# Five unread products in TensorE's first pauses, and the score buffers of an attention kernel in a pool of their own

## The chip, the core and the metric

One core of a Trainium2 chip runs the whole program. Its engines are TensorE (PE in the rows; PEld is its loading of stationary operands), VectorE (DVE), ScalarE (ACT), GpSimd (POOL) and SyncE (SP), whose queue starts the transfers. The metric is the time of one execution on the device, in microseconds, as the median of several runs.

## The reference

An attention block with decay feeds two feed-forward blocks, all in fp32 (4 batches, 8 heads, 576 positions, head size 64):

```python
scores = scale * np.matmul(q, k.transpose(0, 1, 3, 2))
decay = cum[:, :, :, None] - cum[:, :, None, :]      # cum = cumsum(log(clip(f)))
scores = np.where(causal, -1000000000.0, scores + decay)
attn = softmax(scores)                               # with row maximum, + 1e-9 in the sum
x = matmul(attn, v)                                  # to 2304 tokens x 512
h = x @ w_in;  x = (h * np.cos(h)) @ w_out           # 512 -> 2048 -> 512
g = x @ w_gate; out = (silu(g) * (x @ w_val)) @ w_out2   # 512 -> 1536 -> 512
```

## The kernel before

**Attention** goes over 16 pairs of heads, with the two heads of a pair on the two halves of the partitions. The scores of a pair are made in five row tiles (`emit_s`, `S0` to `S4`, lines 311 and 314): pair 0 straight from the loaded fp32 `raw` tile, the others from a high and a low part (`xqh`, `xql`) that GpSimd splits off; a product of `sel` and `cs` adds the decay. VectorE adds the mask and takes the row maximum (`M`, line 338), ScalarE takes the exponential (`E`, line 345), TensorE transposes the result with the identity `ident` (`T`, line 382), ScalarE and VectorE copy the transposes out of PSUM (`C`, lines 390 and 392), and TensorE multiplies by `v` (`V`, line 403). VectorE scales by the reciprocal row sums into `xp` (`N`, line 414), and a transfer writes `xp` to DRAM as `x1` (line 418).

The order on every engine is a list written out by hand, `SCH`: an entry `S2@2` is step `S2` of the pair two before the one of the present round. In the first rounds most steps have no pair yet, so TensorE has nothing between the scores of pair 0 (`S0 S1 S4`, then `S2 S3`), those of pair 1 and those of pair 2. The four score tiles of PSUM are single, so `S2` waits until the maxima of `S0`, `S1` and `S4` are taken, and the next pair's `S0` until those of `S2` and `S3` are. The transposes, the product with `v`, and the two products with which the program begins (`WARM`, line 264) take their results from one pool, `ps_t`, of four PSUM buffers, in turn.

At the same time weights are loaded and turned from 64 to 32 bits and into high and low parts (`w_step`, the `stage` pool).

**The two blocks after it** work on chunks of 384 tokens. For the first, `in1` makes `h` from 12 products (`mm_in`, line 198), ScalarE rounds it to `n` (line 536), VectorE forms `a` and `r`, ScalarE takes the sine, VectorE multiplies, and `gh` and `gl` (lines 548 and 107) are its two parts; `out1` (line 563) multiplies them by the second weight, two steps behind `in1`. A chunk's input is loaded by `load_x` into `xl` and split by GpSimd into `xh` and `xl` (lines 110 and 107). The second chunk's load is held by a gate: a one-element copy from `rs` of the last pair into `xl`. The weights of this stage are still being turned while it runs.

**Memory.** Pools are stacked from the left (`wa`, then `ap1`, `ap2`, `stage` of attention) and from the right (`xpool` of the first chunk). When attention ends its pools are closed, and the next pools (`stage2`, `wb` on the left; `xpool2`, `mp2` with `n`, `mp3` with `r`, `gh`, `gl`, then `pp`, `wst` on the right) lie over the same bytes. A tile waits for the last users of the bytes under it.

Of the kernel before, what the change touches and what calls it, by code (L numbers as in the profile page):

```python
# [9 lines left out]
F32 = mybir.dt.float32  # L10
F32R = mybir.dt.float32r
# [7 lines left out]
B, H, S, D = 4, 8, 576, 64  # L19
NH = B * H  # L20
NPAIR = NH // 2
# [10 lines left out]
RWB = 3  # L32
# [3 lines left out]
WARM = 2  # L36
# [19 lines left out]
SIDE_R = "right"  # L56
# [33 lines left out]
def body(ctx: ExitStack, tc: tile.TileContext, qk, v, f, w_in, w_out, w_gate, w_val, w_out2, mask_c, ident_c, sel_c, out):  # L90
    nc = tc.nc
    PE, ACT, DVE, POOL, SP = nc.tensor, nc.scalar, nc.vector, nc.gpsimd, nc.sync
# [13 lines left out]
    def subtract(eng, o, a, b):  # L106
        eng.tensor_tensor(out=o, in0=a, in1=b.bitcast(F32), op=ALU.subtract)  # L107

    def pool_round(o, a):
        POOL.tensor_scalar(out=o, in0=a, scalar1=1.0, scalar2=0.0, op0=ALU.mult, op1=ALU.add)  # L110
# [96 lines left out]
    def load_x(pool, src, t0, n, g=False, later=False):  # L207
        xl = pool.tile([128, KD, n], F32R, tag="xl", name="xl")
        xh = pool.tile([128, KD, n], F32R, tag="xh", name="xh")
        if g:  # L210
            gate(xl[0:1, 0, 0:1])
        SP.dma_start(out=xl.bitcast(F32), in_=src[:, :, t0:t0 + n])
        for kk in range(KD):
            if later:
                xsplit.append((xh, xl, kk))
            else:
                split_x(xh, xl, kk)
        return xh, xl


    xpools = [None, None]
    xpools[0] = ctx.enter_context(tc.tile_pool(name="xpool", bufs=1, side=SIDE_R))
    actx = ExitStack()
    ap1 = actx.enter_context(tc.tile_pool(name="ap1", bufs=1))
    mask = ap1.tile([128, S], F32, name="mask")
    ident = ap1.tile([128, 128], F32, name="ident")
    ap2 = actx.enter_context(tc.tile_pool(name="ap2", bufs=2))
    stages[0] = actx.enter_context(tc.tile_pool(name="stage", bufs=2))
    pctx = ExitStack()
    ps_t = ctx.enter_context(tc.tile_pool(name="ps_t", bufs=PST, space=PSUM))  # L230
# [4 lines left out]
    raws = {}  # L235

    def load_pair(i):
        raws[i] = ap1.tile([128, 2, S], F32, tag="raw", name="raw", bufs=RWB)
        SP.dma_start(out=raws[i], in_=qk[i])

    def prep_v(i):
        vt_t[i] = ap2.tile([128, 5, 2, D], F32, tag="vt", name="vt", bufs=VTB)
        SP.dma_start(out=vt_t[i], in_=v[i])
# [4 lines left out]
    Ps = [ap1.tile([128, PW], F32, name=f"P{k}") for k in range(PB)]  # L248
    fo, lc = Ps[2:4]
    lf, ones, cum = fo[:, 0:S], fo[:, S:2 * S], lc[:, 0:S]  # L250
    cs = ap1.tile([128, S], F32R, name="cs")
    selr = ap1.tile([128, NPAIR + 1], F32, name="selr")
    sel = ap1.tile([128, NPAIR, 128], F32R, name="sel")
    SP.dma_start(out=lf, in_=f)
    load_pair(0)
    SP.dma_start(out=selr, in_=sel_c)
    SP.dma_start(out=mask, in_=mask_c)
# [1 line left out]
    SP.dma_start(out=ident, in_=ident_c)  # L259
    DVE.memset(ones, 1.0)  # L260

    for k in range(WARM):
        idle = ps_t.tile([128, 512], F32, tag="t", name="t")
        PE.matmul(idle, lhsT=ones[:, 0:128], rhs=ones[:, 0:512], start=True, stop=True)
    DVE.memset(hpi, float(np.pi / 2))
    ACT.activation(out=hpi[:, 0:1], in_=ones[:, 0:1], func=AF.Ln)
    ACT.activation(out=hpi[:, 0:1], in_=ones[:, 0:1], func=AF.Identity, scale=float(np.pi / 2))
# [20 lines left out]
    xq = {}  # L288

    def emit_q(i, k):  # L290

        if k == 0:
            xq[i] = [ap2.tile([128, 2, S], F32R, tag=a, name=a) for a in ("xqh", "xql")]
        (h, l), x = xq[i], raws[i]
        if k % 2 == 0:
            pool_round(h[:, k // 2], x[:, k // 2])
        else:
            subtract(POOL, l[:, k // 2], x[:, k // 2], h[:, k // 2])

    def s_mm(i, t, at, lo, n):  # L300

        q0, rows, _, _ = QT[t]
        if i:
            xh, xl = xq[i]
            parts = (xh, xh), (xl, xh), (xh, xl)
        else:
            parts = (raws[i], raws[i]),
        for m, (x, y) in enumerate(parts):
            for e in range(2):
                b = slice(64 * e, 64 * e + 64)  # L310
                PE.matmul(ss[e][:rows, at[0], at[1]], lhsT=x[b, 0, q0:q0 + rows], rhs=y[b, 1, lo:lo + n], start=(m == 0), stop=False)  # L311
        for e in range(2):
            b = slice(64 * e, 64 * e + 64)
            PE.matmul(ss[e][:rows, at[0], at[1]], lhsT=sel[b, i, :rows], rhs=cs[b, lo:lo + n], start=False, stop=True)  # L314

    def emit_s(i, t):
        if t == 4:
            for h in range(2):
                s_mm(i, 4, (h, slice(0, 288)), 288 * h, 288)
        else:  # L320
            s_mm(i, t, SAT[t], 0, QT[t][2])
# [11 lines left out]
    def emit_m(p, t):  # L333
        if p not in P:
            P[p] = Ps[p % PB]
        q0, rows, ext, c0 = QT[t]
        m1 = S if t else S - 64
        DVE.tensor_tensor_reduce(  # L338
            out=view(P[p][:rows, c0:c0 + ext], t), in0=ss[p % 2][:rows, SAT[t][0], SAT[t][1]], in1=view(mask[:rows, m1 - ext:m1], t),
            scale=-0.125, scalar=3e38, op0=ALU.add, op1=ALU.min, accum_out=mxt[p % 8][:rows, t:t + 1])  # L340

    def emit_e(p, t):
        q0, rows, ext, c0 = QT[t]
        o = P[p][:rows, c0:c0 + ext]
        ACT.activation(out=o, in_=o, func=AF.Exp, scale=-1.0, bias=mxt[p % 8][:rows, t:t + 1],  # L345
                       accum_out=smt[p // 2 % 3][:rows, p % 2, t:t + 1])
# [30 lines left out]
    def emit_t(p, b):  # L377
        ps = tps[p, b] = ps_t.tile([128, 512], F32, tag="t", name="t")
        for col, t, j in TB[b]:
            q0, rows, ext, c0 = QT[t]  # L380
            k0 = c0 + k_lo(j)
            PE.transpose(ps[:, col:col + 128], in_=P[p][:, k0:k0 + 128], identity=ident)  # L382

    def emit_c(p, b):
        if p not in PT:
            PT[p] = ap2.tile([128, PTW], F32, tag="pt", name="pt", bufs=PTB)
        ps = tps.pop((p, b))
        o = PT[p][:, TB_OFF[b]:TB_OFF[b] + TB_W[b]]
        if PTE[p % 2][b]:
            DVE.tensor_copy(o, ps[:, :TB_W[b]])  # L390
        else:
            ACT.copy(out=o, in_=ps[:, :TB_W[b]])  # L392
# [4 lines left out]
    def emit_pv(i, half):  # L397

        q0, w, blocks = PVH[half]
        ps = pvs[i, half] = ps_t.tile([128, 512], F32, tag="t", name="t")  # L400
        for j, c, o in blocks:
            for e in range(2):
                PE.matmul(ps[64 * e:64 * e + 64, o:w], lhsT=vt_t[i][:, j, e], rhs=PT[2 * i + e][:, c:c + w - o],  # L403
                          start=(j == 0), stop=(j == blocks[-1][0]))
# [11 lines left out]
    def emit_o(i):  # L416
        b, hp = divmod(i, H // 2)
        SP.dma_start(out=x1[128 * hp:128 * hp + 128, S * b:S * b + S], in_=xp.pop(i))
# [6 lines left out]
    def load_chunk(k, later=False):  # L425
        if k < len(chunks):
            s, c = chunks[k]
            xs[s, c] = load_x(xpools[k % 2], x1v if s == 1 else x2v, c * CH, CH, GX and k == 1, later)

    def op(o, i):  # L430

        if not 0 <= i < NPAIR:
            return
        k, e = o[0], int(o[-1]) if o[-1] in "01" else 0
        p = 2 * i + e
        if o[:2] == "ld":
            i > 1 and load_pair(i)
        elif o == "lv":
            prep_v(i)
        elif k == "S":  # L440
            emit_s(i, int(o[1]))
        elif k == "M":
            emit_m(p, int(o[1]))
        elif k == "E":
            emit_e(p, int(o[1]))
        elif k == "T":
            emit_t(p, int(o[1]))
        elif k == "C":
            emit_c(p, int(o[1]))
        elif k == "r":  # L450
            emit_recip(i, o[1])
        elif k == "V":
            emit_pv(i, e)
        elif k == "N":
            emit_n(i, e)
        elif o == "xo":
            emit_o(i)
        elif o == "xk":
            if i == XL:
                load_chunk(0, True)  # L460
            elif i >= XP:
                for _ in range(min(XN, len(xsplit))):
                    split_x(*xsplit.pop(0))
        elif o == "wd":
            i < SA and w_load(i)
        elif k == "w":
            i < SA and w_step(i, int(o[1]))
        elif k == "q":
            i and emit_q(i, int(o[1]))
        else:  # L470
            raise ValueError(o)
# [29 lines left out]


    rctx = ExitStack()
    xpools[1] = rctx.enter_context(tc.tile_pool(name="xpool2", bufs=1, side=SIDE_R))
    mp2 = rctx.enter_context(tc.tile_pool(name="mp2", bufs=2, side=SIDE_R))
    mp3 = rctx.enter_context(tc.tile_pool(name="mp3", bufs=3, side=SIDE_R))
    pctx2 = ExitStack()
    pp = pctx2.enter_context(tc.tile_pool(name="pp", bufs=1, side=SIDE_R))
    wst = pctx2.enter_context(tc.tile_pool(name="wst", bufs=2, side=SIDE_R))
# [121 lines left out]
    for i in range(len(steps) + LAG):  # L631
        if i < len(steps):
# [7 lines left out]
            k = chunks.index((s, c)) + 1  # L640
# [103 lines left out]
```

## Time and profile before

| | us |
|---|---|
| median of 3 runs | 1048.92 (1047.85 to 1051.23) |
| the profiled execution | 1050.59 |
| its span, first to last instruction | 1048.8 |
| TensorE busy in it | 1030.2 (98%) |

Attention takes about the first 192 us, the first block runs to about 595 us, the second to the end. The rows quoted below are of one profiled execution; times in them start at the first instruction.

### The profile page before, as it was taken

To read this page: it belongs to the slowest core of one execution; us is meant where nothing else is said; L and a number is where in the kernel's file an instruction comes from. 1 tells how busy PE (TensorE), PEld (TensorE's weight loads), DVE (VectorE), ACT (ScalarE), POOL (GpSimd) and SP (SyncE) were. 2 spreads that over 40 slices of the span, in tenths; PEclk is the share of its full clock that TensorE was granted. 3 is DMA by queue.
4 is the path that set the end of the run, shared out by engine and by line. 5 is a ranking of instruction groups with operands and counts; after the bars stand their busy time and mean duration, and the time that the engine had idled before them with its cause. 6 is when DMAs were issued, how large, how long until landed. Compare 5 with 4: busy or idle time off the path is not lost.

```text
span 1048.8 us, 16876 instructions
## 1 busy us (share of the span) xinstructions
PE 1030.2 (98%) x6448; PEld 964.9 (92%) x6448; DVE 548.6 (52%) x1261; ACT 436.2 (42%) x1019; POOL 314.1 (30%) x332
## 2 busy tenths in 40 slices
PE   6999999899999999999999999999999999999998
PEld 4787877799999999999999999999999999999997
DVE  4788887698898788888855411211111211111111
ACT  5888888355655555555543311111111211211211
POOL 3565655242242141321402211311311311311111
PEclk8999999999999999999999999999999999999999
DMA  4566664533465545555368630100100100000000
GB/s 156 188 187 210 189 196 144 169 107 105 161 212 204 187 154 189 191 188 172 143 231 290 235 128 1 61 1 1 61 1 1 61 1 28 34 1 1 31 1 31
DMA packets 44817, 121.91 MB, mean 116 GB/s; under 512 B 4512, under 2 KB 16064, under 8 KB 44736
## 3 DMA queue, kind: packets, MB, share of 16 engines
q1 hardware_dynamic: 44736, 120.83, 34.2%
q8 instruction: 51, 0.84, 0.3%
q14 instruction: 30, 0.25, 0.1%
HBM read 86.12 MB, written 34.68 MB: 115 GB/s over the span
## 4 chain that ended last, share of the span: by engine, by line
PE 94%; DVE 2%; ACT 2%; DMA 1%; POOL 1%; issue 0%; SPq 0%; ACTq 0%
PE h L198 46%; PE t L563 16%; PE t L597 14%; PE t L382 5%; PE s L311 4%; PE t L403 4%; PE t L566 2%; PE s L314 1%; DMA vt<-in_v_dram 1%; ACT P L345 1%; DVE P L338 0%; DMA selr<-in_sel_dram 0%; DMA x<-xp 0%; DVE r L542 0%; ACT pt L392 0%
## 5 line engine op out<-in xcount | busy, mean ns | idle before, releaser
L198 PE MATMUL h<-xh,w 128*128 128x384 f32 x1920 | 374.4, 336 | 0.5 <-POOL xh L110 0.5
L198 PEld LDWEIGHTS h<-xh,w 128*128 128x128 f32 x1920 | 338.9, 188 | 7.4 <-POOL xh L110 0.8
L198 PE MATMUL h<-xl,w 128*128 128x384 f32 x960 | 205.1, 334 | 0.0
L585 DVE TENSOR_TENSOR r<-h,r 128x384 f32<-128x384 f32 x72 | 40.1, 557 | 289.8 <-ACT r L584 289.8
L107 POOL TENSOR_TENSOR gl<-r,gh 128x384 fp32r<-128x384 f32 x72 | 72.7, 1010 | 333.5 <-ACT gh L520 333.5
L198 PEld LDWEIGHTS h<-xl,w 128*128 128x128 f32 x960 | 169.8, 188 | 0.0
L563 PE MATMUL t<-gh,w 128*128 128x384 f32 x704 | 136.5, 334 | 1.6 <-ACT gh L548 1.6
L597 PE MATMUL t<-w,gh 128*128 128x512 f32 x432 | 134.1, 392 | 0.0
L563 PEld LDWEIGHTS t<-gh,w 128*128 128x128 f32 x704 | 123.3, 188 | 2.0 <-ACT gh L548 2.0
L584 ACT ACTIVATE r<-h 128x384 f32<-128x384 f32 x72 | 35.4, 492 | 213.0 <-PE h L198 203.6
L544 ACT ACTIVATE r<-r,hpi 128x384 f32<-128x384 f32 x96 | 59.3, 618 | 125.1 <-DVE r L542 123.9
L520 ACT CAST gh<-r 128x384 fp32r<-128x384 f32 x72 | 36.9, 513 | 150.5 <-DVE r L586 150.5
L107 POOL TENSOR_TENSOR wst<-ta,wst 128x512 fp32r<-128x512 f32 x36 | 46.5, 1292 | 154.0 <-ACT wst L173 97.9
L597 PEld LDWEIGHTS t<-w,gh 128*128 128x128 f32 x432 | 80.1, 188 | 13.3
L345 ACT ACTIVATE P<-P,mx 128x576 f32<-128x576 f32 (+4 forms) x160 | 87.5, 547 | 5.7 <-DVE mx L338 5.7
L597 PE MATMUL t<-w,gl 128*128 128x512 f32 x216 | 85.2, 396 | 0.0
L540 DVE SCALAR_TENSOR_TENSOR a<-n,h 128x384 f32<-128x384 int32 x96 | 53.9, 562 | 57.9 <-ACT n L536 56.9
L338 DVE CUSTOM_DVE_ANT_0 P<-s,mask 128x576 f32<-128x576 f32 (+4 forms) x160 | 68.2, 483 | 17.0 <-PE s L314 17.0
L536 ACT ACTIVATE n<-h 128x384 int32<-128x384 f32 x96 | 47.1, 490 | 68.4 <-PE h L198 56.7
L586 DVE TENSOR_TENSOR r<-h,r 128x384 f32<-128x384 f32 x72 | 40.2, 558 | 67.4 <-PE h L198 67.4
L563 PE MATMUL t<-gl,w 128*128 128x384 f32 x352 | 75.2, 334 | 0.0
L563 PEld LDWEIGHTS t<-gl,w 128*128 128x128 f32 x352 | 62.3, 188 | 0.0
(80 smaller groups left out, 1320.3 us busy)
## 6 DMA issues: line engine op xcount, KB each, us to landing
w_d<-wst SPq DMA_DIRECT2D x36, 512.0 KB
w<-w_d SPq DMA_DIRECT2D x36, 512.0 KB
wraw<-in_w_out_dram SPq DMA_DIRECT2D x28, 512.0 KB
raw<-in_qk_dram SPq DMA_DIRECT2D x16, 576.0 KB
xl<-x SPq DMA_DIRECT2D x12, 768.0 KB
wraw<-in_w_in_dram SPq DMA_DIRECT2D x16, 512.0 KB
x<-part SPq DMA_DIRECT2D x8, 768.0 KB
wraw<-in_w_gate_dram SPq DMA_DIRECT2D x12, 512.0 KB
```

What stands on the lines that cost most here:

```text
L107: eng.tensor_tensor(out=o, in0=a, in1=b.bitcast(F32), op=ALU.subtract)
L198: PE.matmul(ps, lhsT=w[:, a, 128 * kk:128 * kk + 128], rhs=b[:, kk], start=(n == 0), stop=(n == 3 * KD - 1))
L311: PE.matmul(ss[e][:rows, at[0], at[1]], lhsT=x[b, 0, q0:q0 + rows], rhs=y[b, 1, lo:lo + n], start=(m == 0), stop=False)
L338: DVE.tensor_tensor_reduce(out=view(P[p][:rows, c0:c0 + ext], t), in0=ss[p % 2][:rows, SAT[t][0], SAT[t][1]], in1=view(mask[:rows, m1 - ex ...
L345: ACT.activation(out=o, in_=o, func=AF.Exp, scale=-1.0, bias=mxt[p % 8][:rows, t:t + 1], accum_out=smt[p // 2 % 3][:rows, p % 2, t:t + 1])
L382: PE.transpose(ps[:, col:col + 128], in_=P[p][:, k0:k0 + 128], identity=ident)
L403: PE.matmul(ps[64 * e:64 * e + 64, o:w], lhsT=vt_t[i][:, j, e], rhs=PT[2 * i + e][:, c:c + w - o], start=(j == 0), stop=(j == blocks[-1][0]))
L536: ACT.activation(out=n, in_=h, func=AF.Copy, scale=INV2PI, bias=0.25)
L540: DVE.scalar_tensor_tensor(out=a, in0=n, scalar=-PI2_HI, in1=h, op0=ALU.mult, op1=ALU.add)
L544: ACT.activation(out=r, in_=r, func=AF.Sin, bias=hpi, scale=1.0)
L563: PE.matmul(acc[m][:, :CH], lhsT=wo[:, q, 128 * m:128 * m + 128], rhs=x, start=(j == a and n == 0), stop=False)
L597: PE.matmul(acc[m], lhsT=a[:, s], rhs=w[:, b], start=(j == 0 and n == 0), stop=(j == J2 - 1 and n == 2))
```

## The change

The helper `warm` makes products whose results nobody reads. It replaces the loop of the two first products, and is called in addition after three steps of the scores: one product after `S4` of pair 0, two after `S3` of pair 0, two after `S3` of pair 1. The new products have the identity as stationary operand and 448 columns of the mask as moving one, and are fp32. `mask`, `raw`, `cs`, `selr`, `sel`, `xqh` and `xql` move from `ap1` and `ap2` into a new pool `aps`, stacked behind `ap2`; their sizes and numbers stay. On the right `mp2` and `mp3` are taken before `xpool2` and no longer after it.

```diff
     ap1 = actx.enter_context(tc.tile_pool(name="ap1", bufs=1))
-    mask = ap1.tile([128, S], F32, name="mask")
     ident = ap1.tile([128, 128], F32, name="ident")
     ap2 = actx.enter_context(tc.tile_pool(name="ap2", bufs=2))
+
+    aps = actx.enter_context(tc.tile_pool(name="aps", bufs=1))
+    mask = aps.tile([128, S], F32, name="mask")
     stages[0] = actx.enter_context(tc.tile_pool(name="stage", bufs=2))
...
-        raws[i] = ap1.tile([128, 2, S], F32, tag="raw", name="raw", bufs=RWB)
+        raws[i] = aps.tile([128, 2, S], F32, tag="raw", name="raw", bufs=RWB)
...
-    cs = ap1.tile([128, S], F32R, name="cs")
-    selr = ap1.tile([128, NPAIR + 1], F32, name="selr")
-    sel = ap1.tile([128, NPAIR, 128], F32R, name="sel")
+    cs = aps.tile([128, S], F32R, name="cs")
+    selr = aps.tile([128, NPAIR + 1], F32, name="selr")
+    sel = aps.tile([128, NPAIR, 128], F32R, name="sel")
...
-    for k in range(WARM):
-        idle = ps_t.tile([128, 512], F32, tag="t", name="t")
-        PE.matmul(idle, lhsT=ones[:, 0:128], rhs=ones[:, 0:512], start=True, stop=True)
+    def warm(n, a, b):
+        for k in range(n):
+            idle = ps_t.tile([128, 512], F32, tag="t", name="t")[:, :b.shape[-1]]
+            PE.matmul(idle, lhsT=a, rhs=b, start=True, stop=True)
+
+    warm(WARM, ones[:, 0:128], ones[:, 0:512])
...
-            xq[i] = [ap2.tile([128, 2, S], F32R, tag=a, name=a) for a in ("xqh", "xql")]
+            xq[i] = [aps.tile([128, 2, S], F32R, tag=a, name=a, bufs=2) for a in ("xqh", "xql")]
...
+    WAIT = {("S4", 0): 1, ("S3", 0): 2, ("S3", 1): 2}
+
     def op(o, i):
...
             emit_s(i, int(o[1]))
+            warm(WAIT.get((o, i), 0), ident, mask[:, 0:448])
...
     rctx = ExitStack()
-    xpools[1] = rctx.enter_context(tc.tile_pool(name="xpool2", bufs=1, side=SIDE_R))
     mp2 = rctx.enter_context(tc.tile_pool(name="mp2", bufs=2, side=SIDE_R))
     mp3 = rctx.enter_context(tc.tile_pool(name="mp3", bufs=3, side=SIDE_R))
+    xpools[1] = rctx.enter_context(tc.tile_pool(name="xpool2", bufs=1, side=SIDE_R))
```

## Rows read from the trace of the kernel before

**Rows 1.** The page: span, and the granted clock in 40 slices

```profile
span 1048.8 us, 16876 instructions
...
PEclk8999999999999999999999999999999999999999
```

**Rows 2.** What TensorE waited for: us in total, times, longest us

```profile
PE s L311 <- DVE mx L338: 4.5, 2, 2.4
PE s L311 <- POOL xql L107: 2.2, 1, 2.2
...
PE t L563 <- ACT gh L548: 1.6, 1, 1.6
...
PE h L198 <- POOL xh L110: 0.5, 1, 0.5
```

**Rows 3.** Windows of 1 us: engines' busy time, granted clock, DMA share, GB/s

```profile
14.00:15.00 1.00, 1.00 (x8) 0.64 (x6) 0.00 (x0) 0.85 (x4) 0.92 (x2) 0.60 0.52 97
...
24.00:25.00 1.00, 1.00 (x9) 0.96 (x8) 0.48 (x4) 0.81 (x2) 0.00 (x0) 0.78 0.09 16
...
31.00:32.00 1.00, 1.00 (x15) 1.00 (x15) 0.62 (x2) 1.00 (x4) 0.00 (x0) 0.63 0.07 10
...
34.00:35.00 1.00, 1.00 (x8) 1.00 (x7) 1.00 (x7) 0.45 (x1) 1.00 (x2) 0.66 0.03 12
```

**Rows 4.** TensorE's timeline: start, us, instruction, count [idle before it, releaser]

```profile
1.50 3.78 PE L264 MATMUL t<-P 128*128 128x512 f32 x4 [1.50 <-DVE hpi L265]
...
13.51 0.81 PE L311 MATMUL s<-raw 64*128 64x320 f32 x4 [2.36 <-DVE mx L338]
...
18.62 0.32 PE L311 MATMUL s<-xqh 64*64 64x64 f32 x2 [2.17 <-DVE mx L338]
...
30.63 0.24 PE L311 MATMUL s<-xqh 64*64 64x64 f32 x2 [2.18 <-POOL xql L107]
```

**Rows 5.** The chain that ended last, 0 to 45 us: start, us, what

```profile
9.93 0.24 PE s L314 x2
...
14.59 1.49 PE s L311 x4
...
20.99 0.24 PE s L314 x2
...
22.19 2.46 PE t L382 x11
...
24.76 2.10 PE t L382 x19
...
44.47 0.13 PE s L314 x2
```

**Rows 6.** VectorE's timeline, 29 to 33 us

```profile
30.40 0.08 DVE L338 DVE_READ_ACCUMULATOR2_ANT mx<- 128x1 f32 x1
...
31.00 0.62 DVE L390 COPY pt<-t 128x448 f32<-128x448 f32 x1
```

**Rows 7.** ScalarE's timeline, 23 to 33 us, first copy and last exponential

```profile
23.06 0.48 ACT L392 COPY pt<-t 128x384 f32<-128x384 f32 x1 [2.78 <-PE t L382]
...
32.60 0.18 ACT L345 ACTIVATION_READ_ACCUMULATOR P<-P,mx 128x1 f32 x1
```

**Rows 8.** ScalarE's timeline and the chain, 190 to 200 us

```profile
195.73 0.49 ACT L536 ACTIVATE n<-h 128x384 int32<-128x384 f32 x1 [11.75 <-DMA x<-xp]
...
192.44 3.19 DMA x<-xp
...
198.69 0.49 ACT gh L548
```

**Rows 9.** TensorE's timeline, 193 to 200 us

```profile
193.25 1.55 PE L198 MATMUL h<-xh,w 128*128 128x384 f32 x8
...
199.22 1.68 PE L563 MATMUL t<-gh,w 128*128 128x384 f32 x8 [1.65 <-ACT gh L548]
```

**Rows 10.** GpSimd's timeline, its last weight work of attention

```profile
188.02 1.27 POOL L107 TENSOR_TENSOR w<-ta,w 128x512 fp32r<-128x512 f32 x1
```

## The prediction

> **What bounds the kernel now.** The page first: the span is 1048.8 us and the row of TensorE's granted clock is at its top in every slice but the first [rows 1]. The profiled execution took 1050.59 us, 1.8 us more than its span; the three timed runs have a median of 1048.92 us, 1.67 us under it, and lie 3.4 us apart. The list of what TensorE waited for shows how little idle time is left: two pauses of together 4.5 us after VectorE's row maxima, one of 2.2 us put down to GpSimd, 1.6 us after ScalarE's `gh`, 0.5 us after GpSimd's `xh` [rows 2]. The first three lie in the first 31 us (2.36 us before 13.51, 2.17 us before 18.62, 2.18 us before 30.63) [rows 4]. They are the pauses that the change fills; the last two lie where attention ends.
>
> [...] The first 10 us print 1.00, but the durations say otherwise: a 288-column step of `cs` takes 0.24 us at 9.93, as it does at 20.99 under 0.50, and 0.13 at 44.47 under 1.00 [rows 5]. So the program starts at the lower level, and the record begins later.
>
> The third pause is put down to GpSimd's `xql`, but VectorE's last maximum of the second pair ends at 30.48, 0.15 us before TensorE starts at 30.63 [rows 4, 6], as in the two pauses that are put down to VectorE. All three pauses are VectorE's work on scores; its length doesn't depend on TensorE's clock, so a pause stays as long when TensorE is faster.
>
> **The change: what the products cost.** Each is an fp32 product of 448 columns; there is one after the large scores of pair 0, two after the last scores of pair 0, two after those of pair 1. [...] The products write buffers of the transposes' pool of four. In the third pause the two oldest are those of the third- and fourth-last transposed blocks; the copy that is late, on VectorE at 31.0 [rows 6], belongs to the last block and isn't theirs. [...]
>
> **What the clock gives back.** If a pause is mostly work, the fall after it should not come. From 14.2 to 16.45 the rest of pair 0's scores ran at half speed (the 448-column step alone 1.49 us, [rows 5]): 2.25 us, of which half, 1.1, comes back. From 18.62 to 24.4 TensorE worked 5.8 us at half speed, pair 1's scores and the first transposes (11 of them took 2.46 us, the 19 across and after the rise 2.10, [rows 5]): 2.9 back. From 31.3 to 34.7 3.4 us: 1.7 back. Sum 5.7 us.
>
> What is late next: ScalarE. Its copies of pair 0's transposes and then its exponentials of pair 1 run nearly unbroken from 23.06 to 32.78 [rows 7], 9.7 us. Its first copy would start at about 19.8 (1.1 us earlier by pair 0's scores, 1.75 by pair 1's, 0.45 by a block transposed at full speed) and the last exponential end at 29.5 at the latest. TensorE, which got to pair 2's scores at 30.63, gets there at 26.6, and with 1.9 to 2.0 us for them at full speed to the transposes that need that exponential at 28.6. So between 0 and 0.9 us is given back there; since part of ScalarE's 9.7 us is waiting for transposes at half speed, I take 0.4: 5.7 - 0.4 = 5.3 us. After that the chain of waits is TensorE's alone to the end of attention, so what is won early is kept. Bounds: 5.7 if ScalarE gives nothing back, 0 if the clock takes no notice.
>
> **What the new order of the buffers gives.** This is no cost of an instruction but of who lies where. Attention's pools are closed and the next stage's tiles are put over them. Adding up the sizes, the first `n` tile of the first product stage lies over the end of the last `xp` buffer, by some 480 bytes. The trace agrees: ScalarE stands still for 11.75 us until `x<-xp` has landed and starts `n` at 195.73, with the transfer from 192.44 on [rows 8], though the 12 products that make its input ended at about 193.3, where the next group starts [rows 9]. From `n` to `gh` (198.69 to 199.17) it is 3.4 us, and TensorE stands 1.65 us until 199.22 [rows 8, 9]. With `mp2` and `mp3` taken first from the right, `n`, `r`, `gh` and `gl` come over the weight staging and the end of the score pool: the last user of the first is GpSimd's `w` at 188.02 to 189.29 [rows 10], of the second the last pair's scores, made before all of that pair's transposes. Then `n` starts at about 193.35, `gh` is there at 196.8, before TensorE has run out of products at 197.57, and the 1.65 us are gone. The 0.5 us behind `xh` [rows 2] is a piece of the second chunk that GpSimd splits behind weight work which VectorE and ScalarE hand it; with these 2.4 us earlier and TensorE only 1.65 earlier, it goes too. The second chunk's tile moves over the score buffers, free far earlier, but its load is still held by the gate copy from `rs`, so it can't run into the last transfers of attention. The queue of SP keeps its order. Sum 2.1 us; bounds 0 (another late tile under `n` or `r`) and 2.1. I take 2.1, since every wait that I can name under the new places ends 4 us before `n`.
>
> Sum: 1050.59 - 5.3 - 2.1 = 1043.2 us, 0.55% under the median of the three runs. A measurement of this kernel can tell about 0.3%, 3.1 us; faster begins at 1045.8.
>
> [...]
>
> **The rivals.**
> A, the forecast: the clock is up from the first pause on, and `n` no longer waits: 1043.2 us.
> [...]
> C: the buffers give nothing, because a tile that I count as free is not: 1050.59 - 5.3 = 1045.3 us. Against: the releases listed above.
> [...]
>
> **How the numbers follow.** A 0.52, B 0.18, C 0.13, D 0.10, and 0.07 for what I haven't thought of. The predicted time is A's, 1043.2; its own range is 1041.0 to 1045.0. Lowest: all terms at their upper bounds, 5.7 + 2.1, give 1042.8, and if the timed runs lie 1.7 under the profiled one as they do now, 1041.1; so 1041.0. Highest: B with its whole overrun and C's zero, 1050.59 - 3.1 = 1047.5. That holds A, B and C, over 8 in 10, and leaves D out. Faster by over 0.3%: nearly all of A, most of B and C, 0.70. Slower by over 0.3% would need D and a bad term besides, 0.03. Within 0.3%: 0.27.
>
> **What would show it.** Right: granted clock 1.00 in every step from 11 to 45 us; three groups of 2, 4 and 4 records of the mask product, each ending before VectorE's last maximum; the unbroken stretch of TensorE starting near 17.4 and 26.6 instead of 18.62 and 30.63; `n` starting where the first product group ends, no wait of `out1` for `gh`. [...] A wait of the transposes for ScalarE of more than 0.4 us near 28 would lower the first term.

## The result, and the profile after

| | before | changed |
|---|---|---|
| median, us | 1049.97 (4 runs, 1047.85 to 1051.23) | 1041.23 (4 runs, 1040.24 to 1042.31) |
| ratio, 95% interval | | 0.9917 (0.9901 to 0.9932) |
| the profiled execution, us | 1050.59 | 1040.93 |
| its span, us | 1048.8 | 1039.1 |

The kernel became 8.7 us faster by the medians, 9.7 us by the spans of the two profiles. The forecast was 1043.2 us; the time lies at the lower end of the range, which begins at 1041.0. Over all the runs that were made beside the experiments below, the kernel before has 64 more times, with medians of 1048.6 to 1049.8 us.

What TensorE waited for, of the lines of [rows 2]: the three pauses are down from 6.7 to 1.5 us, and the lines for `gh` and `xh` are gone.

```profile
PE s L316 <- DVE mx L343: 1.0, 2, 0.5
...
PE s L316 <- POOL xql L107: 0.5, 1, 0.5
```

TensorE's timeline of the changed kernel (start, us, instruction, count, in brackets the idle time before it), beside [rows 4]:

```profile
7.53 0.24 PE L319 MATMUL s<-cs,sel 64*64 64x64 f32 x2 [1.96 <-ACT sel L284]
...
10.09 1.86 PE L267 MATMUL t<-mask,ident 128*128 128x448 f32 x2
12.47 0.81 PE L316 MATMUL s<-raw 64*128 64x320 f32 x4 [0.52 <-DVE mx L343]
...
14.31 1.77 PE L267 MATMUL t<-mask,ident 128*128 128x448 f32 x4
16.56 0.24 PE L316 MATMUL s<-xqh 64*64 64x64 f32 x2 [0.48 <-DVE mx L343]
...
23.70 1.77 PE L267 MATMUL t<-mask,ident 128*128 128x448 f32 x4
25.95 0.24 PE L316 MATMUL s<-xqh 64*64 64x64 f32 x2 [0.48 <-POOL xql L107]
...
33.08 3.35 PE L408 MATMUL t<-pt,vt 128*64 128x256 f32 x32
```

One product took 1.86 us at the lower level, two took 1.77 us at the upper one, and each group ends about 0.5 us before the work that the pause waits for. So in this profile the products lie wholly under VectorE's maxima.

The granted clock of the changed kernel in windows of 1 us (engines' busy time, clock, DMA share, GB/s), beside [rows 3]: it is at half only from 8.7 to 12.1 us, and in every later step up to 45 us it is 1.00, where the kernel before has 0.50 for 10 and for 3.4 us. The fall at 8.7 stands behind one more pause, the 1.96 us of waiting for `sel` early in the first scores (before 7.53), which the change leaves as it is. So the clock was already at half when the product of the first pause began, and it came up just behind that product.

```profile
8.00:9.00 1.00, 1.00 (x13) 0.95 (x12) 0.34 (x1) 0.72 (x1) 0.01 (x1) 0.87 0.99 401
...
12.00:13.00 1.00, 0.53 (x6) 0.46 (x6) 0.41 (x4) 0.83 (x3) 1.00 (x1) 0.93 0.00 0
...
14.00:15.00 1.00, 1.00 (x6) 0.49 (x3) 0.58 (x3) 0.05 (x1) 1.00 (x1) 1.00 0.65 166
...
24.00:25.00 1.00, 1.00 (x4) 0.38 (x2) 1.00 (x5) 1.00 (x5) 0.92 (x2) 1.00 1.05 354
...
31.00:32.00 1.00, 1.00 (x12) 0.83 (x11) 0.96 (x3) 1.00 (x4) 0.12 (x1) 1.00 0.48 90
```

The end of attention, in ScalarE's timeline, beside [rows 8]: `n` now waits for TensorE's products, not for a transfer.

```profile
186.36 0.49 ACT L545 ACTIVATE n<-h 128x384 int32<-128x384 f32 x1 [8.45 <-PE h L198]
...
189.31 0.48 ACT L557 CAST gh<-h 128x384 fp32r<-128x384 f32 x1 [0.25 <-DVE h L555]
```

And in TensorE's, beside [rows 9]: the first product of `out1` follows the last `h` without an idle bracket.

```profile
189.49 0.85 PE L198 MATMUL h<-xl,w 128*128 128x384 f32 x4
190.19 1.55 PE L572 MATMUL t<-gh,w 128*128 128x384 f32 x8
```

### The profile page after: what moved, and what is told of

Read it like the earlier page. It is cut to its first block, busy times and chain, and to the rows that moved or that the text cites. A ratio compares the mean times of both kernels' runs of the same rounds, so it can differ in the third digit from the quotient of the medians.

```text
span 1039.1 us, 16892 instructions
## 1 busy us (share of the span) xinstructions
PE 1028.8 (99%) x6458; PEld 960.9 (92%) x6458; DVE 547.0 (53%) x1261; ACT 435.9 (42%) x1019; POOL 314.4 (30%) x332
## 3 DMA queue, kind: packets, MB, share of 16 engines
q1 hardware_dynamic: 44736, 120.83, 34.7%
## 4 chain that ended last, share of the span: by engine, by line
PE 97%; ACT 1%; DVE 0%; DMA 0%; POOL 0%; issue 0%; SPq 0%; ACTq 0%
PE h L198 48%; PE t L572 18%; PE t L606 14%; PE t L387 5%; PE t L408 5%; PE s L316 4%; PE t L575 2%; PE s L319 1%; ACT P L350 1%; DVE P L343 0%; DMA selr<-in_sel_dram 0%; ACT pt L397 0%; ACT sel L284 0%; PE t L366 0%; POOL xql L107 0%
```

## The experiments

Each was timed in alternation with the kernel before; kernels of one group ran on the same chip. Ratios are to the kernel before. Eleven runs were made in three groups, one of them of the changed kernel again.

**First group: the two parts apart, and the two halves of the second part.** Median of the kernel before: 1049.84 us over 33 runs.

The products alone, every buffer where it was:

```diff
+    WAIT = {("S4", 0): 1, ("S3", 0): 2, ("S3", 1): 2}
...
             emit_s(i, int(o[1]))
+            warm(WAIT.get((o, i), 0), ident, mask[:, 0:448])
```

> The five products alone, all buffers where they were before. My theory: the products keep TensorE's clock up and are worth 5 to 6 us, so about 1044.5 us against a median of about 1050 before; granted clock 1.00 from the first pause to 45 us; ScalarE's first n still starts only when the last x<-xp has landed, and TensorE still stands about 1.6 us for gh. Rival (the start's chance and the buffers make the difference, the products little): within 2 us of the kernel before.

Measured: 1045.07 us over 10 runs, ratio 0.9966 (0.9954 to 0.9977), so 3.6 us by the ratio and 4.8 by the medians, a little less than the 5 to 6 us expected. The clock is up from 11.9 us, in the first pause, to 45 us, as expected. Its end of attention is worse than that of the kernel before: ScalarE's timeline has `n` behind the transfer still,

```profile
189.20 0.49 ACT L543 ACTIVATE n<-h 128x384 int32<-128x384 f32 x1 [11.21 <-DMA x<-xp]
```

TensorE's timeline has a longer wait than [rows 9], 2.24 us against 1.65, and a slow group behind it, 2.87 us for eight products that take 1.55 us in the changed kernel:

```profile
192.69 2.87 PE L570 MATMUL t<-gh,w 128*128 128x384 f32 x8 [2.24 <-ACT gh L555]
195.35 1.26 PE L570 MATMUL t<-gl,w 128*128 128x384 f32 x4
```

The windows show why: in this execution the longer wait is one more pause behind which the clock fell, from 192.8 to 196.2 us.

```profile
191.00:192.00 1.00, 0.00 (x0) 0.00 (x0) 0.44 (x1) 0.90 (x2) 0.00 (x0) 1.00 0.00 0
192.00:193.00 1.00, 0.31 (x1) 0.31 (x2) 0.92 (x3) 0.48 (x1) 0.00 (x0) 0.90 0.66 123
193.00:194.00 1.00, 1.00 (x4) 1.00 (x4) 0.69 (x2) 0.28 (x1) 0.00 (x0) 0.50 1.03 381
...
196.00:197.00 1.00, 1.00 (x7) 1.00 (x7) 1.00 (x3) 0.00 (x0) 0.92 (x2) 0.90 0.00 0
```

The new places of the buffers alone:

```diff
-    WAIT = {("S4", 0): 1, ("S3", 0): 2, ("S3", 1): 2}
+    WAIT = {}
```

> The new places of the buffers alone, no new product. My theory: 2.1 us for n and xh, and up to 1.1 us more if the wait of the last product with v for vt is gone because of the places: 1047 to 1048 us; the three pauses and the half-speed stretches behind them as before. Rival (the wait for vt went by chance of the queue): 2 us and a wait for vt of about 1 us still there.

Measured: 1047.75 us over 11 runs, ratio 0.9977 (0.9966 to 0.9987): 2.1 us by the medians, 2.4 by the ratio, as expected. TensorE's timeline has the three pauses of before, and a wait for `vt`:

```profile
13.32 0.90 PE L316 MATMUL s<-raw 64*128 64x320 f32 x4 [2.35 <-DVE mx L343]
...
18.52 0.32 PE L316 MATMUL s<-xqh 64*64 64x64 f32 x2 [2.17 <-DVE mx L343]
...
30.45 0.24 PE L316 MATMUL s<-xqh 64*64 64x64 f32 x2 [2.18 <-POOL xql L107]
...
188.22 3.35 PE L408 MATMUL t<-pt,vt 128*64 128x256 f32 x32 [0.90 <-DMA vt<-in_v_dram]
```

Only the order on the right, with the score buffers back in `ap1` and `ap2`, no product:

```diff
-    xpools[1] = rctx.enter_context(tc.tile_pool(name="xpool2", bufs=1, side=SIDE_R))
     mp2 = rctx.enter_context(tc.tile_pool(name="mp2", bufs=2, side=SIDE_R))
     mp3 = rctx.enter_context(tc.tile_pool(name="mp3", bufs=3, side=SIDE_R))
+    xpools[1] = rctx.enter_context(tc.tile_pool(name="xpool2", bufs=1, side=SIDE_R))
```

> Only the order of the pools on the right is changed; score buffers stay in ap1 and ap2, no product. By the bytes, n now lies over the weight staging and starts as soon as its products end, but the first r lies over the last xp buffer: VectorE's r then waits for x<-xp, and TensorE's wait for gh shrinks from 1.65 to about 0.4 us: 1.2 us won. Rival (the order of the pools is what counts, whatever lies under them): the whole 2 us.

Measured: 1048.98 us over 11 runs, ratio 0.9994 (0.9983 to 1.0004): 0.9 us by the medians where 1.2 were expected, and not clear of nothing by the ratio. Where the wait went is read from the trace. VectorE's timeline, which had no such wait in the kernel before, has `r` behind the transfer:

```profile
192.59 0.56 DVE L547 SCALAR_TENSOR_TENSOR a<-n,h 128x384 f32<-128x384 int32 x1 [1.71 <-ACT n L543]
193.92 0.56 DVE L549 SCALAR_TENSOR_TENSOR r<-n,a 128x384 f32<-128x384 int32 x1 [0.76 <-DMA x<-xp]
```

and TensorE's wait before `out1` is 0.33 us (about 0.4 expected):

```profile
196.39 1.62 PE L570 MATMUL t<-gh,w 128*128 128x384 f32 x8 [0.33 <-issue]
```

By the addresses, the wait went from the tile that lay on the end of `xp` to the next tile that lies there, `r`, 0.76 us: here the bytes counted, not the order of the pools.

Only the score buffers' own pool, the order on the right as before, no product:

```diff
     rctx = ExitStack()
+    xpools[1] = rctx.enter_context(tc.tile_pool(name="xpool2", bufs=1, side=SIDE_R))
     mp2 = rctx.enter_context(tc.tile_pool(name="mp2", bufs=2, side=SIDE_R))
     mp3 = rctx.enter_context(tc.tile_pool(name="mp3", bufs=3, side=SIDE_R))
-    xpools[1] = rctx.enter_context(tc.tile_pool(name="xpool2", bufs=1, side=SIDE_R))
...
+    WAIT = {}
```

(a diff to the changed kernel).

> Only the score buffers' own pool, the order on the right as before, no product. By the bytes, n, r, gh and gl now lie over score buffers and weight staging, nothing late: the whole 2.1 us, no wait of n for a transfer. Rival (the order of the pools is what counts): n waits for x<-xp as before, nothing won.

Measured: 1047.63 us over 11 runs, ratio 0.9982 (0.9971 to 0.9994): 2.2 us by the medians, the same as both halves together. ScalarE's timeline:

```profile
193.59 0.49 ACT L545 ACTIVATE n<-h 128x384 int32<-128x384 f32 x1 [9.59 <-PE h L198]
```

So the pool alone takes the wait away; the new order on the right adds nothing measurable to it.

**Second group: what the products have to be.** Median of the kernel before: 1048.64 us over 17 runs. Diffs are to the changed kernel.

Products of 8 columns:

```diff
-            warm(WAIT.get((o, i), 0), ident, mask[:, 0:448])
+            warm(WAIT.get((o, i), 0), ident, mask[:, 0:8])
```

> The changed kernel with the five products 8 columns wide instead of 448: as many instructions, hardly any work in the pauses. My theory (work in the pauses holds the clock): the clock falls behind the first and third pause as in the kernel before, three pauses of 2.2 to 2.4 us, 1046 to 1048 us. Rival (it is enough that TensorE issues something in the pause): clock at 1.00 and 1042 to 1043 us. Beside it, for the 1 us wait of the last product with v for vt: if it hangs on where TensorE's instructions lie in the program, it is gone here; if it hangs on how early attention ends, it is there as in the kernel before.

Measured: 1046.42 us over 12 runs, ratio 0.9977 (0.9967 to 0.9987), the ratio of the new buffers without any product. In its profile the clock fell at 8.4 us, as it did at 8.7 and 8.3 in the two profiles of the changed kernel, but it came up again at 22.0 instead of 12.1 and 11.7. The windows behind the first pause and at the rise:

```profile
13.00:14.00 1.00, 1.00 (x6) 0.70 (x6) 0.00 (x0) 1.00 (x5) 0.92 (x3) 0.50 0.00 0
...
21.00:22.00 1.00, 1.00 (x10) 0.83 (x8) 0.00 (x0) 0.00 (x0) 0.92 (x2) 0.50 0.00 0
22.00:23.00 1.00, 1.00 (x10) 0.91 (x9) 0.82 (x3) 0.32 (x1) 0.84 (x1) 0.99 0.06 16
```

The expected fall behind the third pause did not come in this profile. With as many instructions in the pauses as the changed kernel, but less work in them (0.59 us instead of 1.86 in the first), this kernel took about 5 us longer, and its clock was at half for 10 us more. The wait for `vt` was there, 1.5 us, with as many instructions as in the changed kernel, so the place of instructions in the program isn't what removes it.

No product in the first pause:

```diff
-    WAIT = {("S4", 0): 1, ("S3", 0): 2, ("S3", 1): 2}
+    WAIT = {("S3", 0): 2, ("S3", 1): 2}
```

> The changed kernel without the product in the first pause; two in the second and two in the third stay. My theory: the first pause is idle for 2.36 us and the clock falls or stays low behind it in most runs; pair 0's last scores run at half speed, the two products in the second pause start at half speed and overrun it by up to 1.1 us; the clock is up from about 17 to 20 us on: 1043 to 1044 us. Rival (one product of 0.8 to 1.7 us in the first pause does nothing): 1041.2 us like the changed kernel.

Measured: 1043.17 us over 6 runs, ratio 0.9951 (0.9937 to 0.9965). TensorE's timeline: the pause, and the two products behind it that start at half speed, 2.52 us instead of 1.77:

```profile
11.84 0.81 PE L316 MATMUL s<-raw 64*128 64x320 f32 x4 [2.34 <-DVE mx L343]
...
14.57 2.52 PE L267 MATMUL t<-mask,ident 128*128 128x448 f32 x4
```

The clock fell at 12.7 and was up at 16.1, a little earlier than I had put it; 1.7 to 1.9 us slower than the changed kernel by the medians, within the 1043 to 1044 us expected.

Twice as many products:

```diff
+    WAIT = {("S4", 0): 2, ("S3", 0): 4, ("S3", 1): 4}
```

> Twice as many products, 2, 4 and 4. At full speed a pair took 1.77 us in the changed kernel and left 0.48 us of the pause; four take 3.5 us and overrun by 1.3 us in the second and third pause each, two in the first take 1.8 to 3.7 us against 2.4 us: 0 to 1.3. My theory (the pauses are the cover of the products): 2.6 to 3.9 us slower than the changed kernel, 1044 to 1045 us, the clock as in it. Rival (VectorE or ScalarE hide the overrun, since they set the pace early on): within 1 us of the changed kernel.

Measured: 1043.41 us over 6 runs, ratio 0.995 (0.9936 to 0.9963), 1.9 to 2.2 us slower than the changed kernel. TensorE's timeline has the next scores directly behind the products, 3.21 us after the products' start where it was 2.25, so 0.96 us of overrun in the second pause and as much in the third:

```profile
13.81 3.27 PE L267 MATMUL t<-mask,ident 128*128 128x448 f32 x8
17.02 0.24 PE L316 MATMUL s<-xqh 64*64 64x64 f32 x2
```

The overrun goes into the time about one for one: in the profiles 1.9 us of it, less the 0.5 by which the second scores of pair 0 begin earlier here (11.97 against 12.47), stand against spans 1.3 us apart. It is smaller than expected because four products in a row took 3.27 us here, not twice 1.77.

Three products at the very start and two in the first pause:

```diff
-WARM = 2
+WARM = 3
...
-    WAIT = {("S4", 0): 1, ("S3", 0): 2, ("S3", 1): 2}
+    WAIT = {("S4", 0): 2, ("S3", 0): 2, ("S3", 1): 2}
```

> The changed kernel with three products at the very start instead of two, and two in the first pause instead of one. The third takes 1.7 us at half speed and ends at about 7.0 us, before the first scores' operand is there at 7.5 us, so it costs nothing. My theory: the clock is up before pair 0's scores, which then take 1.8 instead of 2.5 to 3.5 us: 0.5 to 1.5 us faster than the changed kernel, about 1040 us, with less spread. Rival (the scores wait for VectorE and ScalarE at the start, or the clock comes up no earlier): within 0.5 us of the changed kernel.

Measured: 1040.27 us over 6 runs, ratio 0.9921 (0.9908 to 0.9935), and all six within 0.28 us, 1040.11 to 1040.39. TensorE's timeline: the third product ends before the scores' operand is there, and the scores that took until 10.09 in the changed kernel's first profile end at 9.4. The wait for `sel` before 7.53, behind which the clock fell there, is filled.

```profile
1.50 5.49 PE L267 MATMUL t<-P 128*128 128x512 f32 x6 [1.50 <-DVE hpi L270]
...
9.40 1.77 PE L267 MATMUL t<-mask,ident 128*128 128x448 f32 x4
```

It is the fastest kernel here, 1.0 to 1.2 us under the medians of the changed one. The intervals of the ratios overlap, since those carry the spread of the kernel before; its own six times lie under all five of the changed kernel's in the third group, and under three of its first four (the fourth, 1040.24, lies among them).

**Third group: the changed kernel again, and two parts left out.** Median of the kernel before: 1048.78 us over 14 runs.

> The changed kernel once more, beside the two below on one chip: 1041 to 1042 us, ratio 0.991 to 0.993; in its profile the clock stays up from the first pause on, and TensorE has no wait for gh. Open beforehand: whether the last product with v waits for vt (it did in six of the ten profiles so far, 0.8 to 1.5 us, the changed kernel's not among them). If the missing wait belongs to the change, it is missing again; if it is chance, it may be there.

Measured: 1041.5 us over 5 runs (1041.17 to 1042.05), ratio 0.9929 (0.9914 to 0.9944). The clock is up from 11.7 us on; no wait for `gh`, none for `vt`.

No products in the third pause:

```diff
+    WAIT = {("S4", 0): 1, ("S3", 0): 2}
```

> The changed kernel without the two products in the third pause. My theory: TensorE idles 2.2 us there, the clock falls behind it in most runs, and pair 2's scores and the transposes behind them run 3.4 us at half speed: 0 to 1.7 us slower than the changed kernel, 1042.5 us in the middle, with more spread. Rival (after ten us of unbroken work the clock no longer falls): the same as the changed kernel.

Measured: 1044.18 us over 6 runs (1042.9 to 1044.71), ratio 0.9951 (0.9936 to 0.9966), 2.7 us slower than the changed kernel, more than expected. Its profile doesn't show what I meant to see: the third pause is there in TensorE's timeline,

```profile
13.56 1.44 PE L316 MATMUL s<-raw 64*128 64x320 f32 x4 [0.55 <-DVE mx L343]
...
17.05 1.77 PE L267 MATMUL t<-mask,ident 128*128 128x448 f32 x4
...
28.68 0.24 PE L316 MATMUL s<-xqh 64*64 64x64 f32 x2 [2.18 <-POOL xql L107]
...
30.62 1.42 PE L387 MATMUL t<-ident,P 128*128 128x128 f32 x11
```

but the 11 transposes behind it take 1.42 us, as at full speed in the changed kernel. In this execution (1044.71 us) the loss lies elsewhere, and three pieces make up the 3.8 us between the spans. The first scores ran at half speed, so that the second ones begin at 13.56 instead of 12.47: 1.1 us. Pair 0's last scores ran at half speed too, to 17.05, 3.49 us instead of 1.84: 1.65 us. And the last product with `v` waited 1.0 us for `vt`. The record of the granted clock prints 1.00 all the while; the durations show the half speed (0.81 us for the four 320-column products at 12.47 in the changed kernel, 1.44 here). Up to the third pause this kernel is the changed one, so the product in the first pause doesn't bring the clock up early in every execution. Whether the other five executions fell to half speed behind the third pause isn't known, so this run doesn't settle what that pause is worth.

Three products at the start, none in the pauses:

```diff
-WARM = 2
+WARM = 3
...
+    WAIT = {}
```

> The new buffers, three products at the very start, none in the pauses. My theory: pair 0's first scores run at full speed (1 to 1.5 us won), but the first pause is idle for 2.4 us, the clock falls behind it, and the half-speed stretches come as before: 1046 to 1047 us, 5 to 6 us behind the kernel with products at the start and in the pauses. Rival (once up, the clock stays up): 1041 us.

Measured: 1045.26 us over 8 runs (1042.73 to 1046.93), ratio 0.9964 (0.9951 to 0.9977), 5.0 us behind the kernel with products at the start and in the pauses, and a little under the 1046 to 1047 us expected. The windows show a fall at 17.3, behind the second pause, and one at 27.5, behind the third:

```profile
17.00:18.00 1.00, 1.00 (x14) 1.00 (x14) 0.00 (x0) 0.73 (x3) 0.19 (x1) 0.64 0.33 131
...
27.00:28.00 1.00, 1.00 (x18) 1.00 (x20) 0.96 (x2) 1.00 (x5) 0.00 (x0) 0.76 0.08 15
28.00:29.00 1.00, 1.00 (x12) 1.00 (x12) 0.00 (x0) 1.00 (x4) 0.00 (x0) 0.50 0.47 70
```

The first pause, 2.34 us idle, let it pass this time. So the clock, up in the first scores (192 columns of `cs` in 0.38 us at 7.96, where the kernel before took 0.64 at 8.27), didn't stay up without the products; it fell behind the second and the third pause, where the profile before has its falls behind the first and the third, at 14.2 and 31.3.

## Why the prediction was right, step by step

Case A came, with the sign, the mechanisms and the range right and the size 2 us short. The two profiles are compared stretch by stretch: 1.0 us at the start, 5.2 from there to the first product with `v`, 1.0 from there to the last one, where the wait for `vt` is gone, and 2.4 at the end of attention, together the 9.7 us of the spans. One sign was missed: the clock was to be at 1.00 from 11 us on and is so from 12.1.

**The products cost nothing: right.** By the two 512-column products at half speed, 3.78 us in [rows 4], my estimate was 1.89 x 448 / 512 = 1.65 us for one at half speed and as much for two at full speed; they took 1.86 and 1.77, 13% and 7% more, and still ended inside the pauses. Where the doubled products overran two pauses by 0.96 us each, the kernel was 1.9 to 2.2 us slower. The 1.1 us of overrun in the sum for the upper end of the range (two at half speed, 3.3 us by the same estimate, in 2.17) no run shows: the two that began at half speed, in the run without the first product, took 2.52 us, and the next scores began 2.45 us after their start, where it was 2.25 in the changed kernel.

**The clock gives back 5.3 us: right, 5.2 measured.** In the profile before it fell at 14.2 and 31.3, 0.7 us after the pauses that end at 13.51 and 30.63, and was at half to 24.4 and 34.7. From the second scores of pair 0 to the first product with `v` it was 25.8 us (13.51 to 39.31) and is 20.6 (12.47 to 33.08). Its end before, in TensorE's timeline:

```profile
39.31 3.35 PE L403 MATMUL t<-pt,vt 128*64 128x256 f32 x32
```

By pieces: pair 0's last scores 2.94 to 1.84 us, 1.1 as forecast; pair 1's scores and transposes 9.83 to 7.14, 2.7 instead of 2.9; pair 2's stretch 8.68 to 7.13, 1.55 instead of 1.7; each of the last two pauses 0.07 longer. The 0.4 us that ScalarE should have kept back weren't: its copies start at 19.07 and its exponentials end at 28.07, 9.0 us against 9.7 in [rows 7], while TensorE starts the transposes at 27.87 without a wait of its own. The two misses cancel. For the third pause the evidence is a count: none of the six profiles with full products there has a fall behind it, and five of the seven without have one (the other two are those of 8 columns and of no products in the third pause).

The second of those rises, at 34.7, came 3.4 us after the fall, but TensorE had worked without a pause for 4.1 us by then, from 30.63 on; the first, at 24.4, came after 5.8 us, from 18.62 on. In case B, with the clock at half behind the first pause, the rise would by these two come between 17.6 and 19.3 us, 4.1 to 5.8 after 13.51 (an estimate).

**The buffers give 2.1 us: right.** 2.1 us alone by the medians; in the profiles the stretch from the end of the last product with `v` to the products that finish the first partial sum (lines 566 and 575) is 37.5 us before and 35.1 after, 2.4. The pair of half changes agrees with the reason: in each of these kernels the tile that waits for the transfer is the one that by the addresses lies over `xp`, and with the score buffers in a pool of their own neither `n` nor `r` waits for it. The 0.5 us for `xh` are less sure: the wait is gone in both profiles of the changed kernel and with the buffers alone, but stands with 0.3 us in the run with products at the start only, which has the same buffers.

**What the sum left out.** Two things that the two profiles differ in besides. First, 1.0 us at the very start: the second scores of pair 0 begin at 12.47 instead of 13.51, because the first scores, which lie before any new product, ran partly at full speed in this execution. That looks like chance and not the change: in the second profile of the changed kernel they begin at 12.96, without products in the third pause at 13.56, and in that of `right_order_only`, which has no product, at 11.68. Second, 1.1 us: the last product with `v` no longer waits for `vt`. In TensorE's timelines, before and changed:

```profile
188.47 3.35 PE L403 MATMUL t<-pt,vt 128*64 128x256 f32 x32 [1.08 <-DMA vt<-in_v_dram]
...
181.23 3.35 PE L408 MATMUL t<-pt,vt 128*64 128x256 f32 x32
```

I had this line before me in the list of waits and left it out of the sum as untouched. It is absent from both profiles of the changed kernel and of the three others that have full products in all three pauses, and present (0.7 to 1.5 us) in the eight others. It doesn't hang on the buffers and not on the count of instructions; what brings the transfer in time isn't settled. It is issued no earlier: in both kernels 1.15 us before the last but one group of products with `v` begins (182.51 before 183.66, 176.42 before 177.57). It is the transfer itself that takes less, 4.8 us at most instead of 5.8.

That the time still fell inside the range, 0.2 us above its lower end, is in part luck. That end allowed for timed runs 1.7 us under the profiled one; after the change the median is 0.3 us above it, and these two unforecast gains took the place of the allowance.

**The two parts together.** Apart they give 0.9966 and 0.9977, together 0.9917 and 0.9929, some 1.5 to 2.7 us more than the product of the two, 0.9943. By the intervals only the larger of the two is clear of the noise, and barely, so that the parts help each other is likely and not shown by the times. One profile shows a way in which they could. The products alone bring attention's end forward, but `n` keeps waiting for `x<-xp`, TensorE's wait grows to 2.24 us, and in that profile the clock fell behind it. I had added the terms as independent.

**The rivals.** B has the clock fall behind the first pause in spite of its product, which by the estimate above fills 0.83 us of 2.36 at full speed. That shows in neither profile of the changed kernel. But B isn't refuted. In both profiles the clock was at half already when the product began, so whether one product at full speed, 0.9 us in 2.4, holds the clock was seen nowhere. Two held it (in the runs with twice as many products and with three at the start, 0.64 and 0.65 us of the pause left); with none it fell in one profile and stayed up in another (products at the start only). And in the run without products in the third pause, the same kernel up to there, pair 0's last scores stayed slow in spite of the product, until about 17 us, as B has it. C, buffers that give nothing, is refuted by the buffers alone, 2.1 us. D, products that run at half speed and overrun the second and the third pause, is refuted by the clock: two took 1.77 us there and left 0.48. Falls stand behind pauses of 2.2 to 2.4 us in the profile before (2.36 and 2.18) and in six of the experiments. In the two profiles of the changed kernel the fall stands at 8.7 and 8.3 us and the rise at 12.1 and 11.7. With the clock up from before the first scores and work in every pause the six times lay within 0.28 us, where the kernel before spreads over 3 to 6 us and the changed one over 0.9 to 2.1.

## What to carry to other kernels

Where TensorE has short pauses that no reordering can fill, look at the granted clock in the microseconds behind them, and at the durations of equal steps: here half-speed work behind the three pauses cost 5.2 us beside the 6.7 us of the pauses. Products that nobody reads cost nothing here where they ended 0.5 us before the pause did, and 1.9 to 2.2 us where they overran two pauses by 0.96 us each; size them at the speed at which they'll run. Where a stage's first tile waits for a transfer it doesn't use, add up the addresses: put the buffers whose last reader is early under the tiles that are needed first (2.1 us here). And when one wait is removed, go through the list for every other wait near the same place and ask whether it shrinks or grows; two were changed here, one of them for the worse until the second part of the change took it away.

## What the runs showed of the hardware

The clock fell behind pauses of 2.2 to 2.4 us (the profile before and six of the experiments), though not behind each of them in each run: the third pause let it pass in the run without products there (2.18 us idle) and in that with 8 columns (1.64 us idle), the first in the run with products at the start alone (2.34 us). Behind the wait early in the first scores it fell in four profiles (waits of 1.96 to 2.12 us); in three others (1.5 to 1.95 us) the first scores behind it ran at full speed throughout. Five products of 8 columns in the same places had no measurable effect on the time: the ratio is 0.9977, as it is with the new buffers and no product. In the profile before the record of the granted clock prints 1.00 in every step up to 14 us, while the durations say half speed (0.24 us for 288 columns at 9.93, [rows 5]); in the run without products in the third pause it prints 1.00 in every step up to 46, while pair 0's last scores took 3.49 us instead of 1.84. There the durations have to be read. That most of the 3 to 6 us by which runs of the kernel before differ from each other comes from when the clock rises and falls in the first 35 us is my estimate, from one comparison: with the clock up before the first scores and work in every pause, six runs lay within 0.28 us.
